# Attention outputs in two one-bank PSUM tiles, even transposes drained by two engines, later casts, and own slots for two early snapshots

## The chip, the cores and the metric

The kernel runs on one core of a Trainium2 chip. The metric is the device time of one execution in microseconds (us). Before the change the median of three runs is 999.97 us (998.2 to 1002.94). The engines are PE (TensorE), DVE (VectorE), ACT (ScalarE), POOL (GpSimd) and SP (SyncE, which here only issues DMAs). Each runs its own list of instructions in order and waits on semaphores for the others.

## The reference, cut to what matters

```
B, H, S, D = 4, 12, 448, 64
scores = q @ k.T / sqrt(D) - log(S);  attn = sigmoid(scores);  o = attn @ v        # 48 heads
x = o, heads joined                                                                # 1792 x 768
h = x @ w_in  (768 -> 2048);  g = elu(h);          x = g @ w_out  (2048 -> 768)    # first MLP
h = x @ w_in2 (768 -> 2048);  g = h - tanh(h);     out = g @ w_out2                # second MLP
```

All inputs are float32. The result has to be close to the fp32 one, so matrix products in the kernel are made from pairs of a rounded high part (type fp32r) and a low part that is the rest.

## The kernel before, in words

There are three stages, one behind the other: attention (0 to about 166 us), the first MLP, the second MLP. The two MLPs are nearly all of the time.

**Attention.** The 48 heads are 24 pairs, and a round m handles the pairs 2m (even) and 2m+1 (odd). For each pair k and q are loaded and transposed by PE through an identity (`transpose`, L325 to L329) into PSUM, copied to `plain` in SBUF (`drain`, L340 on ACT, L342 on DVE), rounded to a high part (`hi`, L352 on ACT for even pairs, L354 on DVE for odd ones) and a low part (`lo`, L358, DVE); both lie in the tile `e`. Three score groups of 18 matmul records follow (`s`, L377), each read by one sigmoid (`sig`, L398, ACT) that writes `an`. A remaining strip of both pairs has its own scores (`sr`, L388), sigmoid (`sig_rest`, L394) and value product (`pvr`, L415, in `pv_rest`). The value products (`pv`, L404) take 12 records for each pair, and `xdone` (L426, DVE) copies an output out of PSUM into x, which lies in R0a, R0b, R1a, R1b. PE's order in a round is: scores of the even pair, transposes of the next even and the next odd pair, scores of the odd pair, `pvr`, `sr` of the next round, `pv` of the even pair, `pv` of the odd pair.

PSUM in this stage: three tiles of two banks each form a ring (`ring`, L432 and after) that scores, odd transposes and `sr` use in turn. A fourth two-bank tile, tagged "o", is used in turn by the even transposes (`t_flat`, L316) and by the outputs of both pairs of a round (L408 and after: one half each). The tile framework makes a later writer of a tile wait for earlier readers of the same tile, whichever half they read.

Beside it, the MLP weights, which come in double-width words, are narrowed to float32 (L605 ACT, L608 and L612 DVE), summed (L665) and stored. These jobs load through SP's DMA queue all the time and fill ACT and DVE between the steps above.

**MLP.** Each product is split into blocks and done by seven block products P1 to P7 (a Strassen-Winograd scheme). Operand sums T1 to T4 of x are made by `x_sum` (L766), their high and low parts by `x_head` (L776, ACT) and `x_rest` (L782, DVE); `w_sum` (L725, mostly POOL), `w_head` (L739) and `w_rest` (L742) do the same for weights. `m_p` (L810) are the matmuls. `snap` (L822, ACT) copies a product out of its PSUM bank to SBUF when a later product must use the bank, `h_add` (L827), `g_sum` (L872) combine, `g_a`, `g_b`, `g_c` (L837, L843, L853) are the ELU. A step (i, g, s) is MLP i, block of columns g, half s of the tokens. Snapshots and partial sums live in numbered slots: slots 4 to 6 are `spare`, from 7 on they lie in R1b, 21 and 22 in the tile `first`, 23 to 25 in `second`. `RINGS` (L1227) lists which slots a step may use and `ring` (L1231) takes the one unused for longest. In step (0,0,1) the snapshot of P5, "s5", goes into the slot `i3` of R1b; R1b then still holds part of x, and the snapshot waits until the last `x_rest` that reads it is done.

**What sets the order.** Every operation is given a due time and a list of operations it depends on, and a planner sorts each engine's list by these. In attention the due times are the table `PHASES` (L114) with a period ROUND of 12000 per round. In the MLP they follow from planned costs. `sums_on` (L768) names the engine of an `x_sum`.

Of the kernel before, what the change touches and what calls it, by code (L numbers as in the profile page):

```python
# [16 lines left out]
class Sched:  # L17
# [94 lines left out]
ROUND = 2 * CYCLE  # L112
# [4 lines left out]
    "t": (1950 - ROUND, 2900 - ROUND), "plain": (2850 - ROUND, 3450 - ROUND), "hi": (4350 - ROUND, 5900 - ROUND), "lo": (5250 - ROUND, 6600 - ROUND),  # L117
# [4 lines left out]
SHIFTS = {(0, "ldv"): -12000, (0, "sr"): ROUND - 4700, (0, "sigr"): ROUND - 3900, (0, "ldvr"): -11000}  # L122


@with_exitstack
def kernel(
# [67 lines left out]
    with tc.manual_schedule():  # L194
# [7 lines left out]
        def attention():  # L202
# [76 lines left out]
            def when(kind, n, *rest):  # L279
                at = PHASES[kind]  # L280
# [5 lines left out]
                return n * ROUND + at + (0 if kind in ("s", "sig", "pv") else SHIFTS.get((n, kind), 0))  # L286
# [29 lines left out]
            def t_flat(n):  # L316
                if ("t", n) not in T:
                    p, tag = (pss[ring[("t", n)][0]], "s") if n % 2 else (pso, "o")
                    T["t", n] = p.tile([128, 2, BK], F32, tag=tag, name="sps").rearrange("p a t -> p (a t)")
                return T["t", n]  # L320

            def transpose(n):
                ps = t_flat(n)
                for c in range(3):
                    nc.tensor.transpose(ps[:, DD + c * 128:DD + (c + 1) * 128], kl[:, n % NL, c], ident)  # L325
                if n % 2 == 0:
                    nc.tensor.transpose(ps[:, :DD], krest[n // NR % 2][:, n // 2 % 2], ident)
                for c in range(R):
                    nc.tensor.transpose(ps[:, BK + c * SP:BK + (c + 1) * SP], ql[:, n % NL, c], ident[:SP, :SP])  # L329

            def parts_of(n):
                lo, hi = DD * (n % 2), DD + EW
                return [("ACT", lo, BK), ("DVE", BK, hi)] if n == 0 else [(("DVE", "ACT")[n % 2], lo, hi)]

            def drain(n, x):
                by, lo, hi = parts_of(n)[x]
                at = DD * (n % 2)
                out, in_ = plain[n % 2][:, lo - at:hi - at], t_flat(n)[:, lo:hi]
# [61 lines left out]
            def pv(n, u):  # L400
                m, x = divmod(n, 2)
                a = T.pop(("a", n, u))
                for j in range(2):
                    nc.tensor.matmul(  # L404
                        out=T["o", m][D * j:D * j + D, x, :S], lhsT=vl[m % NVL][:, x, 3 * j + u], rhs=a[:, j], start=False, stop=(u == 2), skip_group_check=True,
                    )

            def pv_rest(m):  # L408
                T["o", m] = pso.tile([128, 2, BK], F32, tag="o", name="pvps")
                a = T.pop(("a", m))  # L410
                for x in range(2):
                    n = 2 * m + x
                    for j in range(2):
                        lanes = slice(64 * x, 64 * x + 64)
                        nc.tensor.matmul(  # L415
                            out=T["o", m][D * j:D * j + D, x, :S], lhsT=vrest[n // NR % 2][lanes, m % (NR // 2), j], rhs=a[lanes, j], start=True, stop=False, skip_group_check=True,
                        )

            def xdone(n):
                b, hp = pairs[n]  # L420
                ps = T["o", n // 2][:, n % 2]
# [57 lines left out]
        def mlp():  # L479
# [288 lines left out]
            def sums_on(i, s, x):  # L768
                return "POOL" if (i, s) == (0, 1) and x in ("T3", "T4") else "DVE"
# [408 lines left out]
            def operands(i, s):  # L1178
# [22 lines left out]
                for x in ORDER:  # L1201
# [18 lines left out]
                    if x in SUMS:  # L1220
# [7 lines left out]
                     "g1": range(4), "gs": (23, 24, 25), "s10": range(4), "s11": (4, "i3", 0, 1, 2, 3), "r1": (5, 6)}  # L1228
            temps_free = {}

            def ring(kind, key, then, i=0):  # L1231
                turns[0] += 1
                slots = [t if isinstance(t, int) else 7 + 4 * i + int(t[1]) for t in RINGS[kind]]
                slot_of[key] = t = min(slots, key=lambda t: (used.get((kind[0], t), 0), slots.index(t)))
                used[kind[0], t] = turns[0]
                return tag_take(f"t{t}", then, stage_frees[1] if t >= 23 else scratch_free[0] if t >= 21 else temps_free["R1b"] if t >= 7 else stage_frees[3] if t >= 4 else before_early)

            def first_products(step):
# [14 lines left out]
                kind, kind_r = (f"s1{s}", "r1") if g == 0 else ("s2", "r")  # L1253
# [222 lines left out]
            for i in range(2):  # L1476
# [4 lines left out]
                for g in range(NG):  # L1481
                    first_weights(i, g)
                    for s in range(2):
                        first_products((i, g, s))
                room["R1b"] = [(0, RAW["R1b"], [d for t in range(7 + 4 * i, 11 + 4 * i) for d in turn_of.get(f"t{t}", [])])]
# [64 lines left out]
```

## Time and profile before

| | |
|---|---|
| runs | 999.97, 1002.94, 998.2 us |
| profiled execution | 998.61 us, its span 996.9 us |
| busy in the span | PE 968.8, DVE 766.8, ACT 603.3, POOL 113.8 us |
| mean granted TensorE clock | 0.996 of full speed |
| PE idle in front of `pv` (L404) | 9.5 us |
| longest wait of PE for ACT | 7.3 us, once, in front of L810 |
| DMA | 218.60 MB, 219 GB/s over the span |

The busy times are sums over the span; where they overlap they don't add up. A wait is named by the engine and the line that released it. Matmuls are pipelined, so the duration of one reaches into the next one, and the spacing of starts is the better price.

### The profile page before, as it was taken

How to read it: one execution, taken by the hardware profiler on the slowest of the kernel's cores; microseconds unless marked ns; L12 is line 12 of the kernel's file. 1: busy time of each engine (PE TensorE's matmuls, PEld its weight loads, DVE VectorE, ACT ScalarE, POOL GpSimd, SP SyncE). 2: the span in 40 equal slices, each digit the busy share in tenths (PEclk: the TensorE clock that was granted, in tenths of full speed). 3: DMA queues.
4: the chain of work that ended last, by engine and by line, in shares of the span. 5: the costliest groups of instructions: out<-in, count | busy, mean ns of one | idle time of the engine just before them, and what ended most of it. 6: DMA issues, size and time to landing. Idle time of an engine off the chain costs nothing.

```text
span 996.9 us, 15482 instructions
## 1 busy us (share of the span) xinstructions
PE 968.8 (97%) x5306; PEld 837.6 (84%) x5306; DVE 766.8 (77%) x1108; ACT 603.3 (61%) x940; POOL 113.8 (11%) x112
## 2 busy tenths in 40 slices
PE   7999999699999999999999998999999999999998
PEld 4555555688888888888899987899888999999998
DVE  4778888977888788778888898877777888666673
ACT  5778778666666677665666564444444565446652
POOL 2212210522222200000000201111111000000000
PEclk9999999899999999999999999999999999999999
DMA  8998870255555579999974725555555994455442
GB/s 252 317 350 299 279 260 35 86 186 193 193 193 188 187 252 353 390 399 370 365 252 148 231 75 180 177 192 185 182 192 188 328 328 135 126 171 175 126 146 85
DMA packets 144574, 218.60 MB, mean 219 GB/s; under 512 B 21424, under 2 KB 102896, under 8 KB 144240
## 3 DMA queue, kind: packets, MB, share of 16 engines
q1 hardware_dynamic: 143232, 217.10, 63.9%
q8 instruction: 41, 0.67, 0.3%
q10 hardware_dynamic: 1264, 0.52, 0.2%
q14 instruction: 37, 0.30, 0.1%
HBM read 142.61 MB, written 74.97 MB: 218 GB/s over the span
## 4 chain that ended last, share of the span: by engine, by line
PE 93%; DVE 3%; DMA 1%; issue 1%; ACT 1%; SPq 1%; POOL 0%; POOLq 0%; DVEq 0%; ACTq 0%
PE psa L810 12%; PE psd L810 11%; PE psx L810 10%; PE psu L965 7%; PE psv L965 7%; PE psw L965 7%; PE psa L965 6%; PE psb L965 6%; PE pvps L404 6%; PE psb L810 5%; PE psy L965 5%; PE sps L377 5%; PE psx L965 3%; PE psd L965 1%; PE pvps L415 1%
## 5 line engine op out<-in xcount | busy, mean ns | idle before, releaser
L398 ACT ACTIVATE an<-sps,bias 128x896 f32<-128x896 f32 x72 | 69.7, 1010 | 27.8 <-PE sps L377 27.5
L937 ACT ACTIVATE XB<-t 128x384 fp32r<-128x384 f32 (+1 forms) x111 | 62.1, 563 | 38.0 <-PE psw L965 11.5
L941 DVE TENSOR_TENSOR XB<-t,XB 128x384 fp32r<-128x384 f32 (+1 forms) x111 | 68.3, 625 | 10.6 <-ACT XB L937 10.5
L725 POOL TENSOR_TENSOR second<-second 128x384 f32<-128x384 f32 x15 | 19.2, 1279 | 500.0 <-DMA t<-x_forms 213.5
L404 PE MATMUL pvps<-an,vl 128*64 128x448 f32 x288 | 59.0, 546 | 9.5 <-DVE R0a L426 4.4
L404 PEld LDWEIGHTS pvps<-an,vl 128*64 128x64 f32 x288 | 19.4, 136 | 48.3 <-issue 32.1
L937 ACT ACTIVATE XB<-spare 128x512 fp32r<-128x512 f32 (+1 forms) x72 | 41.3, 574 | 29.7 <-PE psw L965 11.6
L810 PE MATMUL psa<-XB,W 128*128 128x512 f32 x192 | 54.2, 391 | 0.0
L941 DVE TENSOR_TENSOR XB<-spare,XB 128x512 fp32r<-128x512 f32 (+1 forms) x72 | 44.3, 621 | 10.1 <-ACT XB L937 9.8
L377 PE MATMUL sps<-e 64*128 64x448 f32 x432 | 51.1, 375 | 1.1 <-DVE e L354 0.5
L377 PEld LDWEIGHTS sps<-e 64*128 64x128 f32 x432 | 38.5, 184 | 14.5 <-issue 7.8
L965 PE MATMUL psu<-XB,XB 128*128 128x384 f32 (+1 forms) x192 | 46.3, 348 | 0.0
L965 PE MATMUL psv<-XB,XB 128*128 128x384 f32 (+1 forms) x192 | 46.2, 348 | 0.0
L965 PE MATMUL psw<-XB,XB 128*128 128x384 f32 (+1 forms) x192 | 46.1, 348 | 0.0
L810 PEld LDWEIGHTS psa<-XB,W 128*128 128x128 f32 x192 | 36.0, 188 | 7.5
L839 ACT ACTIVATE spare<-t 128x512 f32<-128x512 f32 (+1 forms) x33 | 19.0, 579 | 36.9 <-DVE t L827 35.9
L725 POOL TENSOR_TENSOR first<-first,second 128x384 f32<-128x384 f32 x30 | 41.0, 1366 | 1.2
L253 POOL COPY first<-raw_qk 128x384 f32<-128x384 f32 (+1 forms) x44 | 27.8, 657 | 106.6 <-PE sps L325 90.6
L810 PE MATMUL psd<-XB,W 128*128 128x512 f32 x144 | 35.6, 391 | 1.5 <-DVE W L742 1.3
L843 ACT ACTIVATE spare<-spare 128x512 f32<-128x512 f32 (+1 forms) x64 | 36.5, 572 | 0.8
L965 PE MATMUL psa<-XB,XB 128*128 128x384 f32 (+1 forms) x156 | 36.9, 347 | 0.0
L965 PE MATMUL psb<-XB,XB 128*128 128x384 f32 (+1 forms) x156 | 36.9, 347 | 0.0
(365 smaller groups left out, 2726.2 us busy)
## 6 DMA issues: line engine op xcount, KB each, us to landing
x_forms<-R1b SPq DMA_DIRECT2D x58, 256.0 KB, 2.0
first<-p_forms SPq DMA_DIRECT2D x36, 384.0 KB, 6.2
t<-x_forms SPq DMA_DIRECT2D x64, 192.0 KB, 3.0
t<-x_forms SPq DMA_DIRECT2D x47, 256.0 KB, 5.0
x_forms<-t SPq DMA_DIRECT2D x44, 256.0 KB, 2.0
x_forms<-R1b SPq DMA_DIRECT2D x58, 192.0 KB, 4.8
first<-in_moe_w_in_dram SPq DMA_DIRECT2D x14, 768.0 KB, 5.3
second<-in_moe_w_in_dram SPq DMA_DIRECT2D x14, 768.0 KB, 6.9
```

Of the source, the lines that this page charges most:

```text
L253: nc.gpsimd.tensor_copy(out=(ql, kl)[w][:, n % NL].rearrange("p c (h d) -> p c h d", h=2), in_=x)
L377: nc.tensor.matmul(out=ps[:, j, :S], lhsT=e[lanes, EW * kz + u * 128:EW * kz + (u + 1) * 128], rhs=e[lanes, EW * qz + KW:EW * qz + EW], st ...
L398: nc.scalar.activation(out=a, in_=T.pop(("s", n, u))[:, :, :S], func=ACTF.Sigmoid, bias=bias, scale=scale)
L404: nc.tensor.matmul(out=T["o", m][D * j:D * j + D, x, :S], lhsT=vl[m % NVL][:, x, 3 * j + u], rhs=a[:, j], start=False, stop=(u == 2), skip ...
L415: nc.tensor.matmul(out=T["o", m][D * j:D * j + D, x, :S], lhsT=vrest[n // NR % 2][lanes, m % (NR // 2), j], rhs=a[lanes, j], start=True, s ...
L725: by.tensor_tensor(out=out, in0=x, in1=y, op=op)
L810: nc.tensor.matmul(out=ps, lhsT=w[wz][:, k0:k0 + 128], rhs=xs[xz][:, kk], start=(opens and n == 0), stop=(n == 3 * KH - 1), skip_group_che ...
L839: nc.scalar.activation(out=r, in_=h, func=ACTF.Tanh)
L843: nc.scalar.activation(out=r, in_=r, func=ACTF.Exp, scale=-1.0)
L937: nc.scalar.activation(out=at_place(og_place[i, s, p, j], 0, i)[:, :HW[s]], in_=T["graw", i, s, p, j], func=ACTF.Copy)
L941: nc.vector.tensor_tensor(out=lo, in0=T.pop(("graw", i, s, p, j)), in1=f(hi), op=ALU.subtract)
L965: nc.tensor.matmul(out=T["o2", tag], lhsT=lhsT, rhs=rhs, start=(p in OPENS and j == 0 and x == 0), stop=(j == NG - 1 and x == 2), skip_gro ...
```

## The change

1. The fourth PSUM tile becomes two tiles of one bank each, "o0" and "o1" (new function `output`). The output of the even pair lies in o0 and that of the odd pair in o1. An even transpose has its k part in o0 and its q part in o1.
2. Even transposes are drained in two parts, 128x512 by ACT and 128x448 by DVE (before: 128x960 by DVE, but for pair 0). Odd ones are still drained by ACT.
3. The due times of `hi` and `lo` move: later for even pairs (from 4350 and 5250 to 6800 and 7700), earlier for odd pairs (from 5900 and 6600 to 4900 and 5500). Pairs 0 and 1 have corrections of their own.
4. The sums T3 and T4 of step (0,1) move from POOL to DVE.
5. The snapshots of step (0,0,1) use a ring of their own, "sa", of slots 4, 21, 22 and 3. "s5" then lies in slot 21 and "s2" in slot 22, both in `first`, which is used by other work afterwards; that work waits for them.

```diff
-    ... "hi": (4350 - ROUND, 5900 - ROUND), "lo": (5250 - ROUND, 6600 - ROUND),
+    ... "hi": (6800 - ROUND, 4900 - ROUND), "lo": (7700 - ROUND, 5500 - ROUND),
+FIRST_PAIRS = {(0, "hi"): -2450, (0, "lo"): -2450, (1, "hi"): 1000, (1, "lo"): 1100}
...
             def t_flat(n):
                 if ("t", n) not in T:
-                    p, tag = (pss[ring[("t", n)][0]], "s") if n % 2 else (pso, "o")
-                    T["t", n] = p.tile([128, 2, BK], F32, tag=tag, name="sps").rearrange("p a t -> p (a t)")
+                    if n % 2:
+                        ps = pss[ring[("t", n)][0]].tile([128, 2, BK], F32, tag="s", name="sps")
+                        T["t", n] = [ps[:, z] for z in range(2)]
+                        T["t", n, "all"] = ps.rearrange("p a t -> p (a t)")
+                    else:
+                        T["t", n] = [output(z) for z in range(2)]
                 return T["t", n]
+
+            def output(x):
+                return pso.tile([128, BK], F32, tag=f"o{x}", name=f"pv{x}")
...
             def parts_of(n):
                 lo, hi = DD * (n % 2), DD + EW
-                return [("ACT", lo, BK), ("DVE", BK, hi)] if n == 0 else [(("DVE", "ACT")[n % 2], lo, hi)]
+                return [("ACT", lo, hi)] if n % 2 else [("ACT", lo, BK), ("DVE", BK, hi)]
...
-                        out=T["o", m][D * j:D * j + D, x, :S], lhsT=vl[m % NVL][:, x, 3 * j + u], ...
+                        out=T["o", n][D * j:D * j + D, :S], lhsT=vl[m % NVL][:, x, 3 * j + u], ...
...
             def xdone(n):
                 b, hp = pairs[n]
-                ps = T["o", n // 2][:, n % 2]
+                ps = T["o", n]
...
             def sums_on(i, s, x):
-                return "POOL" if (i, s) == (0, 1) and x in ("T3", "T4") else "DVE"
+                return "DVE"
...
-                     "g1": range(4), "gs": (23, 24, 25), "s10": range(4), "s11": (4, "i3", 0, 1, 2, 3), "r1": (5, 6)}
+                     "g1": range(4), "gs": (23, 24, 25), "s10": range(4), "s11": (4, "i3", 0, 1, 2, 3), "sa": (4, 21, 22, 3), "r1": (5, 6)}
...
-                return tag_take(f"t{t}", then, ... scratch_free[0] if t >= 21 else ...)
+                return tag_take(f"t{t}", then, ... scratch_free[0] + stage_frees[0] if t >= 21 else ...)
...
-                kind, kind_r = (f"s1{s}", "r1") if g == 0 else ("s2", "r")
+                kind, kind_r = ("sa" if step == (0, 0, 1) else f"s1{s}", "r1") if g == 0 else ("s2", "r")
```

**Where it shows in the lists of instructions.** Lines of the changed kernel are numbered 12 higher from L340 on, so L404 there is L416. On PE, the value products of round 0, from the first output of the odd pair on, in the kernel before; the third row is the one that waits for DVE's copy:

```order
L404 MATMUL pvps<-an,vl_119 64x448 [waits DMAHW7_49]
L404 MATMUL pvps<-an,vl_119 64x448
L404 MATMUL pvps<-an,vl_119 64x448 [waits DVE_49,Activation_49]
L404 MATMUL pvps<-an,vl_119 64x448
L404 MATMUL pvps<-an,vl_119 64x448 [waits Activation_49]
```

and the same place in the changed kernel, where pv_284 is the tile o1:

```order
L416 MATMUL pv_284<-an,vl_119 64x448 [waits DMAHW7_49]
L416 MATMUL pv_284<-an,vl_119 64x448
L416 MATMUL pv_284<-an,vl_119 64x448 [waits Activation_49]
L416 MATMUL pv_284<-an,vl_119 64x448
L416 MATMUL pv_284<-an,vl_119 64x448 [waits Activation_49]
```

The wait for DVE is gone there, and the order of PE's matmuls is the same.

On ACT, one round of attention before (plain_122 is the odd pair's copy, e_83 the even pair's high part):

```order
L398 ACTIVATE an<-sps,bias 128x896 x3
L340 ACTIVATE plain_122<-sps 128x832
L352 ACTIVATE e_83<-plain_121 128x832
L398 ACTIVATE an<-sps,bias 128x896
L605 ACTIVATE XB_71<-XB_71 128x768
L398 ACTIVATE an<-sps,bias 128x896
L394 ACTIVATE ar<-sps,bias 128x896
L398 ACTIVATE an<-sps,bias 128x896
L605 ACTIVATE R1b<-R1a 128x768
```

and in the changed kernel:

```order
L410 ACTIVATE an<-sps,bias 128x896 x3
L352 ACTIVATE plain_121<-pv_359 128x512
L352 ACTIVATE plain_122<-sps 128x832
L410 ACTIVATE an<-sps,bias 128x896
L617 ACTIVATE XB_71<-XB_71 128x768
L410 ACTIVATE an<-sps,bias 128x896
L364 ACTIVATE e_83<-plain_121 128x832
L406 ACTIVATE ar<-sps,bias 128x896
L410 ACTIVATE an<-sps,bias 128x896
L617 ACTIVATE R1b<-R1a 128x768
```

A half drain of the even pair stands in front of the odd pair's drain, and the even pair's cast stands two places further back.

On DVE, the opening of the first MLP before, from the T2 sum on; the last row is the T4 rest, the last reader of x in R1b:

```order
L766 TENSOR_TENSOR R1a<-R1b,R1a 128x3x384
L827 TENSOR_TENSOR t<-t,psb 128x512
L827 TENSOR_TENSOR t<-t,psd 128x512
L827 TENSOR_TENSOR t<-t,psa 128x512
L782 TENSOR_TENSOR XB_1804<-R1a,XB_1804 128x1152
L853 SCALAR_TENSOR_TENSOR t<-spare,t 128x512 x2
L782 TENSOR_TENSOR XB_1804<-R1b,XB_1804 128x1152
L782 TENSOR_TENSOR XB_1804<-R1a,XB_1804 128x1152
L853 SCALAR_TENSOR_TENSOR t<-spare,t 128x512
L872 TENSOR_TENSOR t<-t 128x512
L742 TENSOR_TENSOR e_83<-first,e_83 128x768
L782 TENSOR_TENSOR R1a<-R1b,R1a 128x1152
```

and in the changed kernel, from the rest of T2 on, to the T4 rest and one row more:

```order
L794 TENSOR_TENSOR XB_1858<-R1a,XB_1858 128x1152 [waits Activation_49]
L778 TENSOR_TENSOR R1a<-R1a 128x3x384
L794 TENSOR_TENSOR XB_1858<-R1b,XB_1858 128x1152
L865 SCALAR_TENSOR_TENSOR t<-spare,t 128x512 [waits DVE_49,Activation_49]
L794 TENSOR_TENSOR XB_1858<-R1a,XB_1858 128x1152 [waits Activation_49]
L778 TENSOR_TENSOR R1b<-R1b,R1a 128x3x384
L754 TENSOR_TENSOR e_83<-first,e_83 128x768 [waits DMAHW2_49,PE_49,Activation_49]
L865 SCALAR_TENSOR_TENSOR t<-spare,psa 128x512 [waits Activation_49]
L839 TENSOR_TENSOR spare<-spare,psb 128x384
L794 TENSOR_TENSOR R1a<-R1b,R1a 128x1152 [waits Activation_49]
L839 TENSOR_TENSOR first<-first,psx 128x384 [waits PE_49]
```

Two sums (L778) have come in, and one ELU step (L853) and one `g_sum` (L872) less stand ahead of the T4 rest.

On ACT, the snapshot of P5 before, and what stands ahead of it:

```order
L776 ACTIVATE R1a<-R1b 128x1152 [waits DVE_49,Pool_49]
L843 ACTIVATE spare<-spare 128x512 [waits Activation_49]
L739 ACTIVATE W_1730<-second 128x768 [waits PE_49,Pool_49]
L822 ACTIVATE R1b<-psd 128x384 [waits DVE_49]
L837 ACTIVATE spare<-spare 128x384 [waits DVE_49]
```

and in the changed kernel:

```order
L788 ACTIVATE XB_1858<-R1a 128x1152 [waits DVE_49]
L751 ACTIVATE e_83<-first 128x768 [waits DMAHW2_49,PE_49]
L849 ACTIVATE spare<-psa 128x512 [waits DVE_49]
L834 ACTIVATE first<-psd 128x384 [waits PE_49]
L855 ACTIVATE spare<-spare 128x512 [waits Activation_49]
L834 ACTIVATE first<-psx 128x384 [waits PE_49]
```

The snapshot now goes into `first`, waits for PE alone, and stands ahead of the head of T4 (L788 R1a<-R1b), which follows two rows further on.

## Rows read from the trace of the kernel before

**Rows 1.** The page, part 1: busy us, share of the span, instructions.
```profile
PE 968.8 (97%) x5306; PEld 837.6 (84%) x5306; DVE 766.8 (77%) x1108; ACT 603.3 (61%) x940; POOL 113.8 (11%) x112
```

**Rows 2.** The page, part 5: busy, mean ns | idle before, releaser; the value products.
```profile
L404 PE MATMUL pvps<-an,vl 128*64 128x448 f32 x288 | 59.0, 546 | 9.5 <-DVE R0a L426 4.4
```

**Rows 3.** Timeline of PE in one round: start, duration, instruction [idle before <-releaser].
```profile
51.39 2.09 PE L377 MATMUL sps<-e 64*128 64x448 f32 x18
...
55.10 2.09 PE L377 MATMUL sps<-e 64*128 64x448 f32 x18
...
58.78 3.23 PE L404 MATMUL pvps<-an,vl 128*64 128x448 f32 x16
62.83 1.72 PE L404 MATMUL pvps<-an,vl 128*64 128x448 f32 x8 [0.82 <-DVE R0a L426]
```

**Rows 4.** Timeline of ACT in the same round, from the even pair's sigmoids on.
```profile
52.37 2.81 ACT L398 ACTIVATE an<-sps,bias 128x896 f32<-128x896 f32 x3 [4.17 <-PE sps L377]
55.20 0.87 ACT L340 ACTIVATE plain<-sps 128x832 f32<-128x832 f32 x1
55.97 0.90 ACT L352 ACTIVATE e<-plain 128x832 fp32r<-128x832 f32 x1
```

**Rows 5.** The drains' lines by form: ns min/median/max, starts, forms.
```profile
L340 ACT ACTIVATE plain<-sps x13: 597/871/872, 6.4 to 146.1; 128x832 f32<-128x832 f32 x12, 128x512 f32<-128x512 f32 x1
...
L342 DVE COPY plain<-sps x12: 625/1158/1159, 7.1 to 145.4; 128x960 f32<-128x960 f32 x11, 128x448 f32<-128x448 f32 x1
```

**Rows 6.** Stretches: us, then PE, PEld, DVE, ACT, POOL busy, PEclk, DMA share, GB/s.
```profile
100.00:150.00 50.00, 47.35 (x358) 26.83 (x356) 42.96 (x70) 39.12 (x47) 7.94 (x12) 1.00 0.82 267
12.00:150.00 138.00, 128.97 (x965) 72.41 (x963) 107.46 (x160) 107.57 (x127) 27.07 (x43) 1.00 0.91 302
...
190.00:200.00 10.00, 5.01 (x17) 5.01 (x18) 9.18 (x13) 5.38 (x9) 1.12 (x1) 0.66 0.40 152
```

**Rows 7.** Timeline of PE at the opening of the first MLP.
```profile
181.98 1.75 PE L810 MATMUL psb<-XB,e 128*128 128x384 f32 x9
183.56 1.73 PE L810 MATMUL psd<-R0b,W 128*128 128x384 f32 x9
185.79 1.86 PE L810 MATMUL psx<-XB,W 128*128 128x384 f32 x9 [0.50 <-ACT spare L822]
194.99 1.01 PE L810 MATMUL psd<-XB,R0a 128*128 128x384 f32 x2 [7.35 <-ACT R1b L822]
...
200.31 2.24 PE L810 MATMUL psa<-XA,e 128*128 128x512 f32 x9
202.39 0.51 PE L810 MATMUL psx<-R1a,e 128*128 128x384 f32 x2
```

**Rows 8.** Timeline of DVE there.
```profile
176.17 1.36 DVE L766 TENSOR_TENSOR R1a<-R1b,R1a 128x1152 f32<-128x1152 f32 x1
...
179.24 2.36 DVE L782 TENSOR_TENSOR XB<-R1a,XB 128x1152 fp32r<-128x1152 f32 x1
181.75 4.36 DVE L853 SCALAR_TENSOR_TENSOR t<-spare,t 128x512 f32<-128x512 f32 x2 [0.15 <-ACT spare L843]
...
188.13 2.14 DVE L782 TENSOR_TENSOR XB<-R1a,XB 128x1152 fp32r<-128x1152 f32 x1
...
193.07 1.35 DVE L782 TENSOR_TENSOR R1a<-R1b,R1a 128x1152 fp32r<-128x1152 f32 x1
194.34 0.68 DVE L853 SCALAR_TENSOR_TENSOR t<-spare,psa 128x512 f32<-128x512 f32 x1
...
195.54 0.54 DVE L827 TENSOR_TENSOR spare<-spare,psb 128x384 f32<-128x384 f32 x1
```

**Rows 9.** Timeline of POOL there: its first sum of x, its first sum of weights.
```profile
177.68 2.70 POOL L766 TENSOR_TENSOR R1a<-R1a 128x1152 f32<-128x1152 f32 x1 [41.87 <-DVE R1a L766]
...
184.09 1.47 POOL L725 TENSOR_TENSOR second<-second 128x384 f32<-128x384 f32 x1
```

**Rows 10.** Timeline of ACT there: the snapshot of P5.
```profile
194.45 0.49 ACT L822 ACTIVATE R1b<-psd 128x384 f32<-128x384 f32 x1 [1.67 <-DVE R1a L782]
```

More of the change, by code (lines that the diff above doesn't have):

```diff
@@ L116 @@
     "sr": 6600 - ROUND, "sigr": 7350 - ROUND,
-    "t": (1950 - ROUND, 2900 - ROUND), "plain": (2850 - ROUND, 3450 - ROUND), "hi": (4350 - ROUND, 5900 - ROUND), "lo": (5250 - ROUND, 6600 - ROUND),
+    "t": (1950 - ROUND, 2900 - ROUND), "plain": (2850 - ROUND, 3450 - ROUND), "hi": (6800 - ROUND, 4900 - ROUND), "lo": (7700 - ROUND, 5500 - ROUND),
     "side": (4500 - 2 * ROUND, 6000 - 2 * ROUND), "ldqk": (7000 - 3 * ROUND, 8500 - 3 * ROUND),
@@ L279, in when @@
             def when(kind, n, *rest):
-                at = PHASES[kind]
+                at, first = PHASES[kind], FIRST_PAIRS.get((n, kind), 0)
                 if kind not in ("sr", "sigr", "pvr", "ldk", "ldv", "ldqk1"):
@@ L285, in when @@
                     at = at[rest[0]]
-                return n * ROUND + at + (0 if kind in ("s", "sig", "pv") else SHIFTS.get((n, kind), 0))
+                return n * ROUND + at + first + (0 if kind in ("s", "sig", "pv") else SHIFTS.get((n, kind), 0))
             def loads(m):
@@ L337, in drain @@
                 at = DD * (n % 2)
-                out, in_ = plain[n % 2][:, lo - at:hi - at], t_flat(n)[:, lo:hi]
+                out = plain[n % 2][:, lo - at:hi - at]
+                if n % 2:
+                    in_ = T["t", n, "all"][:, lo:hi]
+                else:
+                    in_ = t_flat(n)[lo // BK][:, lo % BK:(hi - 1) % BK + 1]
                 if by == "ACT":
@@ L404, in pv @@
                     nc.tensor.matmul(
-                        out=T["o", m][D * j:D * j + D, x, :S], lhsT=vl[m % NVL][:, x, 3 * j + u], rhs=a[:, j], start=False, stop=(u == 2), skip_group_check=True,
+                        out=T["o", n][D * j:D * j + D, :S], lhsT=vl[m % NVL][:, x, 3 * j + u], rhs=a[:, j], start=False, stop=(u == 2), skip_group_check=True,
                     )
             def pv_rest(m):
-                T["o", m] = pso.tile([128, 2, BK], F32, tag="o", name="pvps")
                 a = T.pop(("a", m))
@@ L412, in pv_rest @@
                     n = 2 * m + x
+                    T["o", n] = output(x)
                     for j in range(2):
@@ L415, in pv_rest @@
                         nc.tensor.matmul(
-                            out=T["o", m][D * j:D * j + D, x, :S], lhsT=vrest[n // NR % 2][lanes, m % (NR // 2), j], rhs=a[lanes, j], start=True, stop=False, skip_group_check=True,
+                            out=T["o", n][D * j:D * j + D, :S], lhsT=vrest[n // NR % 2][lanes, m % (NR // 2), j], rhs=a[lanes, j], start=True, stop=False, skip_group_check=True,
                         )
@@ L1235, in ring @@
                 used[kind[0], t] = turns[0]
-                return tag_take(f"t{t}", then, stage_frees[1] if t >= 23 else scratch_free[0] if t >= 21 else temps_free["R1b"] if t >= 7 else stage_frees[3] if t >= 4 else before_early)
+                return tag_take(f"t{t}", then, stage_frees[1] if t >= 23 else scratch_free[0] + stage_frees[0] if t >= 21 else temps_free["R1b"] if t >= 7 else stage_frees[3] if t >= 4 else before_early)
             def first_products(step):
@@ L1484, in mlp @@
                         first_products((i, g, s))
+                        if (i, g, s) == (0, 0, 1):
+                            scratch_free[0] += turn_of["t21"] + turn_of["t22"]
                 room["R1b"] = [(0, RAW["R1b"], [d for t in range(7 + 4 * i, 11 + 4 * i) for d in turn_of.get(f"t{t}", [])])]
```

6 lines of the change are left out of this document (3 added, 3 removed).

## The prediction, made before the changed kernel was run

> **What bounds the kernel now.** I read four views in this order. The busy shares: PE works 968.8 of 996.9 us [rows 1], so all that the change can give back is in the 28 us in which PE stands, or in work that PE does at a lower clock. The groups by cost, then, with the idle time in front of each: 9.5 us of PE's idle time stand before the value products and are put down to DVE's copies of attention outputs [rows 2]. The timelines of one round of attention and of the opening of the first MLP: in the round PE stops for 0.82 us between the 16th and the 17th record of the value products, released by DVE's copy of the even pair's output [rows 3]; at the opening it stops once for 7.35 us, released by a snapshot on ACT [rows 7], which waited for a rest on DVE [rows 10]. Last the stretches: from 190 to 200 us the granted clock is 0.66 of the 2.4 GHz, behind that long stop, and DMA is busy for 0.91 of the stretch from 12 to 150 us [rows 6].
>
> **Part 1, two PSUM tiles.** The 17th record writes the odd pair's half while the copy reads the even pair's half. With two tiles the wait has no cause, and the changed list of PE doesn't have it. All ten waits are of this kind, so 9.5 us go [rows 2]. What could be late instead: records 17 to 24 also need the odd pair's second and third sigmoid, which I place with part 2; and the next even transposes need both copies out of the way, as before, with one score group of about 2.1 us [rows 3] between the last value product and them, while such a copy is short beside it. I cost that at nothing; if the cover were gone, a copy's length, about 0.6 us by the 128x448 copy on DVE [rows 5], would come back each round.
>
> **Part 2, drains.** DVE gives up 1158 ns per even pair for 625 ns, off PE's path. ACT takes over a 128x512 drain of 597 ns [rows 5], ahead of the odd pair's drain. One ACT copy hands over to the next 0.10 us before its end (55.20 + 0.87 against 55.97) [rows 4], so the odd drain moves back by about 0.50 us, its end from 56.07 to 56.57. It frees the ring tile for the third score group of the odd pair. Those 18 records begin at 55.10 and take 2.0 us from start to start, a third of it 0.67 [rows 3], so the third group wants to begin at 56.45. Before there is 0.38 us in hand; afterwards about 0.2 us is missing with the semaphore's way: 11 rounds with an odd drain in them, 2.2 us. Bounds: 0, if the three even sigmoids come earlier by the 0.1 to 0.2 that is missing (ACT sits idle up to 4.17 us before them [rows 4], but that idle is PE's pace), and 5.5 us (all of 0.50 in each of 11 rounds). I take 2.2.
>
> **Part 3, later and earlier casts.** The even pair's cast moves behind two sigmoids and a narrowing, at about 59.2 us by adding rows of 0.9 to 1.0 us each; with its low part it is done by about 62 us, against about 63.7 at which the next round would start without the 0.82 us (62.83 + 1.72 - 0.82) [rows 3]. Cost nothing, 1.5 us in hand; without it, each 0.1 us late costs 1.1 us. The third odd sigmoid goes back by the same 0.50 us as the drain; value products that read it are the last four of the 24 and have some 0.8 us in hand. So attention gives 9.5 - 2.2 = 7.3 us, bounded by 9.5 and 9.5 - 5.5 = 4.0, or less if transfers pace it (a rival).
>
> **Parts 4 and 5, the opening of the MLP.** Before, P6 starts at 185.79 and the products are 1.58 us apart (181.98 to 183.56) [rows 7]. P3 has to wait until P5's snapshot has left the bank, and that waits for the rest of T4, which reads R1b and ends at 194.42 [rows 8, 10]. With a slot in `first` it needs PE's product alone. ACT's list has it ahead of T4's head. So P3 follows P6 at 187.37, P7 at 188.95, and the next psa product at 190.53 instead of 200.31 [rows 7]: 9.8 us, of which 7.35 are the stop, and 2.2 the lower clock (P3 and P7 took 200.31 - 194.99 = 5.3 us instead of 3.2).
>
> What is late next is P4, which uses T4's rest (the psx product on R1a at 202.39 [rows 7], after 2.08 us of psa): it is wanted at 192.6. DVE's chain to that rest, counted from the rest at 179.24: it was 15.2 us long [rows 8]. Six POOL operations ran beside it from 177.68 to 191.1 [rows 6, 9], and stretched three rests from 1.35 to 2.14 to 2.36 (together 2.6 us) and the pair of ELU steps from 2 x 0.68 to 4.36 (3.0 us) [rows 8]. Unstretched that is 9.6. Added: two sums at 1.36 [rows 8], 2.7. Less by the order: one ELU step (0.68) and one `g_sum` of the same shape, more one `h_add` of 0.54; together 0.8 off. That is 11.5, without POOL. POOL keeps four weight sums of 1.47 [rows 9], 5.9 us; at the rate seen, 5.6 us of stretch in 13.4 us of POOL, they cost 2.5. The rest of T4 ends at 179.24 + 14.0 = 193.2, and one `h_add` behind it, 0.54, frees psx: 193.8. P4 waits 1.2 us. Bounds of this wait: 0 (no stretch: 191.3) and 4.6 us (each us of POOL one of DVE: 197.2). I take 1.2, so the opening gives 9.8 - 1.2 = 8.6 us, bounded by 9.8 and 5.2.
>
> The row shows that DVE and POOL slow each other but both run: 5.6 us lost to 13.4. The Trainium skill, "SBUF — State Buffer", section "SBUF: two separate sides", says that the port pair shared by VectorE and GpSimd is an exclusive lock and that "the other fully blocks" where VectorE reads two SBUF inputs. By that rule all of POOL's four sums would stand in DVE's way, P4 would wait near the 4.6 us of the upper bound, and the sum would be 986.1 instead of 982.7. The stretch of less than half agrees with turns between two that are both busy as well as with sharing, so the trace doesn't decide it here.
>
> The slots 21 and 22 were free at that time; what uses `first` next is narrowing for weights that are needed later. I cost this at nothing; if it were late, it would show as a wait of PE for a weight rest. The second MLP's opening has the same instructions but for its sums' neighbours: nothing.
>
> **The sum,** against the profiled execution of 998.61 us, which is 1.4 us under the median of 999.97: 998.61 - 7.3 - 8.6 = 982.7. The spread of the three runs, 4.7 us, is about 0.5%, and less than 0.5% I call no change.
>
> **Rivals.**
> - *The opening pays, attention does not.* Transfers run 0.91 of the time from 12 to 150 us at 302 GB/s [rows 6]. If the narrowing jobs that sit between the sigmoids on ACT arrive as late as before in absolute time, ACT stands before them, and the waits move from the copies to the sigmoids. For it: the high share. Against it: from 100 to 150 us the share is 0.82, and PE still stops for copies. Attention then gives 0 to 2 us: 998.61 - 8.6 - 1 = 989.0.
> - *Attention pays, the opening blocks anew.* DVE is the only engine left with the chain to T4's rest; the two sums it takes over come on top, and POOL's weight sums fall in the same time. With the wait of 4.6 us: 986.1; if snapshots and h_adds behind it are held as well and the opening gives nothing, 991.3. I put it at 987. For it: DVE is busy for 9.18 of the 10 us to 200 [rows 6]. Against: POOL's share is cut by more than half.
> - *Slower: the transfers decide all of attention.* 138 us at 302 GB/s are 41.7 MB. In the last 50 us only 267 GB/s came through [rows 6]. If the tighter order of work makes loads and stores meet such that the whole stretch gets 267, those bytes take 156 us: 18 us more, less 8.6 of the opening: 1008. It ends above the time before from a rate of about 284 GB/s on (147 us). Against it: nothing that is transferred changes, and the low rate of the last stretch goes with a share of 0.82, so engines had time left.
> - *The wait is not the false one.* If records 17 to 24 waited in truth for the sigmoid, with the copy only last by little, part 1 gives half, 4.7: 987.3. The released-by column names DVE in all ten, so I fold it into the first.
>
> **How the numbers follow.** The forecast, 982.7, has 0.65; the first rival 0.19, the second 0.12, the slower one 0.04. The forecast's own ends are 998.61 - 9.5 - 9.8 = 979.3 and 998.61 - 4.0 - 5.2 = 989.4. The first rival reaches to about 992. I give 977 to 993: below 979.3 for a change in the clock or in waits that I don't see, above for the first two rivals; this leaves out the slower case and the edges of the others. Faster by over 0.5% means under 995.0: 0.65 + 0.19 x 0.9 + 0.12 x 0.8 = 0.91, and I say 0.90. Within 0.5%: 0.06; slower: 0.04.
>
> **What will show it.** Right: no idle before the value products put down to `xdone`; rounds that had a stop are 0.6 to 0.8 us shorter; the third odd score group waits 0.1 to 0.3 us for ACT's drain; P3 starts within 1 us after P6; the granted clock stays near 1.00 there; P4 waits 0 to 2 us for DVE. Wrong: value products that wait for sigmoids, ACT standing before narrowing with a DMA as releaser, score groups that wait for the even low part, or a stop of over 4 us before P4 or P3.

## The result and the profile after

The changed kernel takes 985.66 us (median of four runs, 983.11 to 987.84) against 999.12 us before (four runs): a ratio of 0.9857 over all runs (0.9865 by the two medians), 95% interval 0.9819 to 0.9896. The profiled execution took 987.84 us, with a span of 985.8 us. The forecast was 982.7 us, so 3 us of the forecast gain are missing, and in the profiled execution 5. The profile shows that this small difference is the rest of two larger ones of opposite sign.

The page of the changed kernel, part 1, answers [rows 1]: PE has lost 12 of its 28 us of idle time.

```profile
PE 969.9 (98%) x5306; PEld 837.6 (85%) x5306; DVE 762.4 (77%) x1110; ACT 610.3 (62%) x951; POOL 107.8 (11%) x110
```

What PE still waits for, all of the changed kernel's span (us in total, times, longest):

```profile
PE psd L822 <- DVE W L754: 2.4, 2, 1.3
PE psy L977 <- ACT XB L949: 2.0, 1, 2.0
...
PE sps L333 <- ACT an L410: 0.9, 1, 0.9
...
PE sps L389 <- ACT plain L352: 0.7, 2, 0.4
```

The copies of attention outputs are not in the list any more, and neither is the 7.3 us wait for the snapshot. In the MLPs two stops are new: one of the two waits for a weight rest (the other, 1.28 us at the opening of the second MLP, was there before), and psy, the first group of output products. In attention, waits of an odd transpose for a sigmoid (`an`) and of the odd score groups for ACT's drain (`plain`) are new, 1.6 us together.

A round of attention on PE (start, duration, instruction), beside [rows 3]: the 24 value products run through, and the odd pair's score group takes 2.18 for 2.09 us. From its start to the start of the next scores, `pv` takes 4.67 us (54.98 to 59.65) instead of 5.70 (58.78 to 64.48 before), so a stop of 0.82 us of idle time cost 1.03.

```profile
47.50 2.09 PE L389 MATMUL sps<-e 64*128 64x448 f32 x18
...
51.20 2.18 PE L389 MATMUL sps<-e 64*128 64x448 f32 x18
...
54.98 4.73 PE L416 MATMUL pv<-an,vl 128*64 128x448 f32 x24
59.65 2.09 PE L389 MATMUL sps<-e 64*128 64x448 f32 x18
```

The opening of the first MLP on PE, beside [rows 7]: P6, P3, P7 (from 179.60), the next psa product and P4 follow without a stop.

```profile
157.29 2.34 PE L822 MATMUL psa<-XA,e 128*128 128x512 f32 x9
...
176.48 1.72 PE L822 MATMUL psx<-XB,W 128*128 128x384 f32 x9
178.04 0.51 PE L822 MATMUL psd<-XB,R0a 128*128 128x384 f32 x2
...
181.16 2.24 PE L822 MATMUL psa<-XA,e 128*128 128x512 f32 x9
183.24 0.51 PE L822 MATMUL psx<-R1a,e 128*128 128x384 f32 x2
```

DVE there, beside [rows 8]: the T4 rest (180.73) ends at 182.08 and the `h_add` that frees psx at 182.54, 0.7 us before P4 starts.

```profile
171.07 2.13 DVE L794 TENSOR_TENSOR XB<-R1a,XB 128x1152 fp32r<-128x1152 f32 x1
173.12 1.35 DVE L778 TENSOR_TENSOR R1a<-R1a 128x1152 f32<-128x1152 f32 x1
...
180.73 1.35 DVE L794 TENSOR_TENSOR R1a<-R1b,R1a 128x1152 fp32r<-128x1152 f32 x1
182.00 0.54 DVE L839 TENSOR_TENSOR first<-first,psx 128x384 f32<-128x384 f32 x1
```

POOL there, beside [rows 9]: its weight sums are over when the first moved sum starts on DVE.

```profile
167.02 1.93 POOL L737 TENSOR_TENSOR second<-second 128x384 f32<-128x384 f32 x1 [35.44 <-DMA second<-kept_wi]
168.91 1.01 POOL L737 TENSOR_TENSOR first<-first,second 128x384 f32<-128x384 f32 x1
169.88 1.01 POOL L737 TENSOR_TENSOR second<-second,first 128x384 f32<-128x384 f32 x1
170.97 1.01 POOL L737 TENSOR_TENSOR first<-first,second 128x384 f32<-128x384 f32 x1
```

**Where the time is, by four marks.** M0 is the first psa product of the first MLP (165.57 before), M1 the psa product behind the opening (200.31 before [rows 7], 181.16 now), M2 the first stop in the second MLP, which every kernel here has (psx waits 0.96 us for a snapshot; the two rows below, before and now). A mark read on PE's timeline in each profile makes the experiments comparable, since PE's order of matmuls from M0 on is the same in all of them.

```profile
601.81 1.84 PE L810 MATMUL psx<-XB,W 128*128 128x384 f32 x9 [0.96 <-ACT R1b L822]
588.81 1.84 PE L822 MATMUL psx<-XB,W 128*128 128x384 f32 x9 [0.96 <-ACT R1b L834]
```

| profile | to M0 | M0 to M1 | M1 to M2 | M2 to the end | span |
|---|---|---|---|---|---|
| before | 165.6 | 34.7 | 401.5 | 395.1 | 996.9 |
| changed | 157.3 | 23.9 | 407.6 | 397.0 | 985.8 |
| difference | -8.3 | -10.9 | +6.2 | +1.9 | -11.1 |

Attention and the opening gave 19.2 us, more than the 15.9 that were forecast. Then 6.2 us were given back in the rest of the first MLP, where the forecast had nothing. This is where, on PE, in the output products:

```profile
378.00 0.84 PE L977 MATMUL psw<-XB,XA 128*128 128x512 f32 x3
380.88 0.49 PE L977 MATMUL psy<-XB,XA 128*128 128x512 f32 x1 [2.03 <-ACT XB L949]
381.61 1.21 PE L977 MATMUL psy<-XB,XA 128*128 128x512 f32 x2 [0.23 <-DVE XB L953]
382.61 1.49 PE L977 MATMUL psa<-XB,XA 128*128 128x512 f32 x3
383.89 1.40 PE L977 MATMUL psb<-XB,XA 128*128 128x512 f32 x3
385.13 0.84 PE L977 MATMUL psy<-XB,XA 128*128 128x512 f32 x3
```

Groups of three are 0.68 us apart, so the last of these rows would start at 378.00 + 4 x 0.68 = 380.72; it starts at 385.13, 4.4 us late. Half of it is the stop. The other half is the clock behind it, granted at 0.71 from 380 to 384 us (PE, PEld, DVE, ACT, POOL busy, PEclk, DMA share, GB/s):

```profile
376.00:380.00 4.00, 2.84 (x13) 2.03 (x11) 1.54 (x4) 1.78 (x3) 0.00 (x0) 1.00 1.03 394
380.00:384.00 4.00, 2.89 (x7) 2.12 (x8) 2.81 (x4) 3.34 (x6) 0.00 (x0) 0.71 1.04 392
```

The other part of the 6.2 us is a stop of psd for a weight rest, 1.07 us of idle time at 214.32, with the matmuls around it 1.6 us (its third record starts at 214.32; 0.23 apart, counted on from the group before, it would be 212.72). The last 1.9 us, behind M2, are no part of the change: they follow from a low clock behind a 1.28 us stop that the kernel before has as well, and the third kernel of the last set, which has attention and opening as before, has them in its profile, while the second profile of the changed kernel does not.

### The profile page after: what moved, and what is told of

It is laid out like the page before. It is cut to its first block, busy times and chain, and to the rows that moved or that the text cites. A ratio compares the mean times of both kernels' runs of the same rounds, so it can differ in the third digit from the quotient of the medians.

```text
span 985.8 us, 15460 instructions
## 1 busy us (share of the span) xinstructions
PE 969.9 (98%) x5306; PEld 837.6 (85%) x5306; DVE 762.4 (77%) x1110; ACT 610.3 (62%) x951; POOL 107.8 (11%) x110
## 4 chain that ended last, share of the span: by engine, by line
PE 93%; DMA 3%; DVE 2%; ACT 1%; SPq 1%; issue 1%; POOL 0%; DVEq 0%; ACTq 0%; POOLq 0%
PE psa L822 13%; PE psd L822 12%; PE psx L822 10%; PE psu L977 6%; PE psv L977 6%; PE psw L977 6%; PE psa L977 6%; PE psb L977 6%; PE psb L822 6%; PE pv L416 5%; PE psy L977 5%; PE sps L389 4%; PE psx L977 3%; PE psd L977 1%; DMA R1a<-in_moe_w_in_dram 1%; PE pv L427 1%
## 5 line engine op out<-in xcount | busy, mean ns | idle before, releaser
L416 PE MATMUL pv<-an,vl 128*64 128x448 f32 x288 | 56.8, 544 | 0.0
L416 PEld LDWEIGHTS pv<-an,vl 128*64 128x64 f32 x288 | 19.5, 136 | 36.5 <-issue 30.7
L254 POOL COPY first<-raw_qk 128x384 f32<-128x384 f32 (+1 forms) x44 | 36.4, 852 | 93.8 <-DMA raw_qk<-in_k_dram 74.2
L977 PEld LDWEIGHTS psu<-XB,XB 128*128 128x128 f32 x192 | 34.7, 188 | 2.1 <-DVE XB L942 0.2
```

Of the source, the lines that this page charges most:

```text
L254: nc.gpsimd.tensor_copy(out=(ql, kl)[w][:, n % NL].rearrange("p c (h d) -> p c h d", h=2), in_=x)
L416: nc.tensor.matmul(out=T["o", n][D * j:D * j + D, :S], lhsT=vl[m % NVL][:, x, 3 * j + u], rhs=a[:, j], start=False, stop=(u == 2), skip_gr ...
L977: nc.tensor.matmul(out=T["o2", tag], lhsT=lhsT, rhs=rhs, start=(p in OPENS and j == 0 and x == 0), stop=(j == NG - 1 and x == 2), skip_gro ...
```

## The experiments

All are edits of the changed kernel unless it is said otherwise. Times are medians of up to five rounds beside the kernel before on the same chip; a ratio is to that kernel, over all runs, and can differ by up to 0.002 from that of the two medians.

**The first set: the changed kernel again, its two halves, and the DMA queue.** Unedited:

> The changed kernel again, for its spread and a second profile. Theory 1 (a new stop behind the first MLP's input products, 2.0 + 0.2 us of idle time before psy and some 2 us at a lower granted clock behind it, gives back part of the gain every time): the stop is there again at about 381 us, and runs lie at 983 to 988. Theory 2 (what was given back is an accident of one execution, the clock above all): the stop or the low clock is missing in this profile, and most runs lie near 982.

Measured: 985.99 us (983.24 to 986.80), ratio 0.9856 (0.9839 to 0.9874). The stop before psy is there, 3.02 us, with the clock at 0.83 from 380 to 390 us. It belongs to the kernel, as theory 1 has it; the 1.9 us behind M2 don't (395.4 here). Runs lie from 983 to 988 in both sets.

Parts 4 and 5 undone:

```diff
-                return "DVE"
+                return "POOL" if (i, s) == (0, 1) and x in ("T3", "T4") else "DVE"
...
-                kind, kind_r = ("sa" if step == (0, 0, 1) else f"s1{s}", "r1") if g == 0 else ("s2", "r")
+                kind, kind_r = (f"s1{s}", "r1") if g == 0 else ("s2", "r")
```

(and the two places where slots 21 and 22 are handed on).

> The changed kernel with the sums T3 and T4 of step (0,1) back on POOL and the two snapshots in the old ring: only the attention parts are left. Theory 1 (attention alone gives about 8.3 us, by the profiles 165.57 to 157.29 at the first MLP product): 990 to 991, and the stop of about 7.3 us before P3 is there, released by the snapshot into R1b. Rival (the two halves overlap: with attention faster the T4 rest comes relatively later and the stop grows): 993 or more, with a stop above 8 us.

Measured: 987.90 us, ratio 0.9887 (0.9869 to 0.9904). That is 2 us better than theory 1, and the rival is out. M0 is at 155.97, the stop before P3 is the old one, and between M1 and M2 there is no stop at all:

```profile
175.59 1.84 PE L822 MATMUL psx<-XB,W 128*128 128x384 f32 x9 [0.26 <-ACT spare L834]
184.79 1.01 PE L822 MATMUL psd<-XB,R0a 128*128 128x384 f32 x2 [7.37 <-ACT R1b L834]
...
189.41 2.24 PE L822 MATMUL psa<-XA,e 128*128 128x512 f32 x9
```

So attention alone carries 12 of the 13.8 us of these rounds (999.75 to 985.99), and the whole of the opening's 10.9 us are worth 2 us in the end.

The kernel before with parts 4 and 5 alone, the same lines the other way round:

> The kernel before with parts 4 and 5 alone (sums on DVE, own slots for the two snapshots). Theory 1 (the opening alone gives about 10.9 us by 200 us, of which the stop behind the input products takes little since PE arrives there less early): 988 to 990. Rival (the sum of the halves is all there is, and the loss at 381 us belongs to this half): 992 to 993, with a stop of 2 us or more before psy.

Measured: 1001.54 us, ratio 1.0002 (0.9987 to 1.0018): nothing, though single runs lie from 995.10 to 1002.56, wider than elsewhere. Theory 1 is wrong by the whole gain. M0 to M1 takes 25.5 us instead of 34.7, as wanted; but M1 to M2 takes 411.0 instead of 401.5, with these two stops:

```profile
226.14 2.32 PE L810 MATMUL psd<-XB,W 128*128 128x512 f32 x7 [2.57 <-DVE W L742]
```

and 2.27 us before psy. PE comes here 12 us later than in the changed kernel, so being early isn't what makes it wait. The rival had the place right (this half) and the size too small.

Double-width w_out loads begun six output units later:

```diff
-                        p, j = divmod(2 + 3 * n, NG)
+                        p, j = divmod(8 + 3 * n, NG)
```

> The changed kernel with the double-width w_out loads of the second MLP begun six output units later (8 + 3n for 2 + 3n). Theory 1 (the load of 128x1536 double words into R1a, issued at 370.87 ahead of three reloads that the first output products need, makes these late): the stop before psy at 381 us goes, and the time is 3 to 4.5 us under the changed kernel's in the same rounds. Rival (DMA is 1.04 busy there, the rate sets when the operands come, whatever the order): the stop stays at 1.5 us or more and the time is within 1 us of the changed kernel's.

Measured: 982.06 us (981.44 to 982.86), ratio 0.9822 (0.9808 to 0.9837); 3.9 us under the changed kernel of the same rounds, and under every run of it. The stop is 0.91 us, and the clock stays at 1.00. In the changed kernel the queue shows why: the 128x1536 load into R1a (768 KB) stands ahead of three of the four reloads of g into t (256 KB each) issued from 370 to 376 us, and ACT's heads wait for those.

```profile
370.00 0.32 SPq L946 DMA_DIRECT2D t<-x_forms  x1
370.87 0.33 SPq L606 DMA_DIRECT2D R1a<-in_moe_w_out_dram  x1
372.36 0.32 SPq L946 DMA_DIRECT2D t<-x_forms  x1
...
374.09 0.32 SPq L946 DMA_DIRECT2D t<-x_forms  x1
```

```profile
377.95 0.63 ACT L949 ACTIVATE XB<-t 128x512 fp32r<-128x512 f32 x1 [2.52 <-DMA t<-x_forms]
...
380.20 0.63 ACT L949 ACTIVATE XB<-t 128x512 fp32r<-128x512 f32 x1 [0.41 <-DMA t<-x_forms]
```

The DMA share is 1.00 to 1.06 in either kernel at this place, so it is the order in the queue that decides, not the rate alone. The kernels with old slots agree: there the same load, the first of w_out into R1a, is issued behind four reloads of g into t. In the kernel without part 5, below, that is 3.4 us ahead of psy, which starts at 382.35 without a stop:

```profile
378.96 0.53 SPq L606 DMA_DIRECT2D R1a<-in_moe_w_out_dram  x1
```

In the changed kernel it is 7.8 us ahead of 378.68, where psy would have started. This version has the lowest median of the study.

**The second set: each part undone by itself.** Part 5 undone, the sums left on DVE (the `kind` line above):

> The changed kernel without part 5: the snapshots of step (0,0,1) in the old ring, the two sums on DVE. Theory 1 (the own slots in `first` hold up the narrowing of the next weights, and that is what the changed kernel pays for later): P3 stands 4 to 5 us, until DVE has done the T4 rest, but the stops at 214 us (weight rest) and 381 us (psy) are gone, and from the first psa product behind the opening to the next MLP's first stop it takes 401 to 402 us as before, not 407 to 409; the time is 984 to 986. Rival (those stops come from PE being early, or from the sums on DVE): they stay, and the time is 988 or more.

Measured: 985.52 us, ratio 0.9866 (0.9852 to 0.9880): the same as the changed kernel. The opening costs three short stops, 4.4 us in all,

```profile
175.87 2.04 PE L822 MATMUL psd<-R0b,W 128*128 128x384 f32 x9 [2.16 <-DVE t L839]
177.71 3.08 PE L822 MATMUL psx<-XB,W 128*128 128x384 f32 x9
181.84 0.62 PE L822 MATMUL psd<-XB,R0a 128*128 128x384 f32 x2 [1.05 <-ACT R1b L834]
...
184.89 0.62 PE L822 MATMUL psx<-XB,R0a 128*128 128x384 f32 x2 [1.22 <-ACT t L834]
```

and M1 to M2 takes 401.5 us, with no stop. Theory 1 holds, but for the form of the stop, which is split in three. With the loads where they are, part 5 is worth nothing: it wins 6.8 us before M1 (30.7 to 23.9) and loses 6.2 to 7.2 behind it.

Part 4 undone, the own slots left (the `sums_on` line above):

> The changed kernel without part 4: the own slots, but the sums T3 and T4 on POOL. Theory 1 (the slots cause the later stops): a weight rest is waited for at 210 to 225 us by 1 us or more and psy by 1 us or more. P3 does not stand; P4 waits 3 to 8 us for the T4 rest, since POOL's sums take 2.7 and 3.8 us beside a busy DVE. Time 988 to 993. Rival (the sums on DVE cause the later stops): no stop at 214 and 381, and a time of 983 to 986.

Measured: 989.41 us, ratio 0.9898 (0.9884 to 0.9911). M1 to M2 takes 407.4 us and psy stops for 2.43; so the slots are what makes psy late, whoever does the sums. (All of its 5.9 us over 401.5 stand here: the 2.43, and slower matmuls behind the stop, at a clock of 0.50 from 384 to 388 us.) The stop for a weight rest is not there, against theory 1; it needs the sums on DVE too. In the opening it is P3 that waits, 3.84 us, and not P4.

The even transposes' k part drained by DVE as well:

```diff
-                return [("ACT", lo, hi)] if n % 2 else [("ACT", lo, BK), ("DVE", BK, hi)]
+                return [("ACT", lo, hi)] if n % 2 else [("ACT" if n == 0 else "DVE", lo, BK), ("DVE", BK, hi)]
```

> The changed kernel with both parts of the even transposes drained by DVE (two copies, 128x512 and 128x448), but for pair 0. Theory 1 (ACT's share makes the odd drain 0.5 us later, for which the third odd score group pays 0.1 to 0.25 us a round, and DVE has room): attention 1 to 3 us shorter, the third group's 18 records take 2.09 again and not 2.18. Rival (DVE's later casts then are late and the even low part holds the next scores): attention 3 us longer or more, PE waiting for DVE e.

Measured: 991.87 us, ratio 0.9925 (0.9913 to 0.9937), 6 us worse, and not by attention: M0 is at 157.0, and it lies between 155.2 and 158.2 in all kernels with two tiles. The odd score group takes 2.28 us in six rounds here, longer than the 2.18 of the changed kernel, so this run doesn't show that ACT's drain is what it pays for. With the old cast times it is 2.18 in most rounds with ACT's drain (the next experiment) and 2.09 in most rounds with DVE's (part 1 alone, in the third set). So the small price of ACT's drain is there with the old cast times; with the new ones DVE's drains are no cheaper, and nothing of either is seen at M0. The 6 us are behind M0: 25.2 to M1, and in M1 to M2, 412.2 us, with a stop of 2.57 for a weight rest at 217.14 and one of 2.23 before psy. The opening parts in the kernel before (first set) have nearly the same two stops, 2.57 and 2.27, and 411.0 us; there DVE drains the even transposes too. The planner sets the first MLP's order from planned costs, and this edit moved it: the lists of DVE and ACT behind M0 are no longer the changed kernel's, but nearly those of that other kernel. Own slots cost 9.5 to 10.7 us behind M1 in these two, 6 to 7 in the kernels with ACT's drains. I did not follow that further. Both theories were about the wrong place.

The old cast times:

```diff
-    ... "hi": (6800 - ROUND, 4900 - ROUND), "lo": (7700 - ROUND, 5500 - ROUND),
+    ... "hi": (4350 - ROUND, 5900 - ROUND), "lo": (5250 - ROUND, 6600 - ROUND),
...
-FIRST_PAIRS = {(0, "hi"): -2450, (0, "lo"): -2450, (1, "hi"): 1000, (1, "lo"): 1100}
+FIRST_PAIRS = {}
```

> The changed kernel with the old due times of hi and lo. Theory 1 (the later even cast takes ACT's time out of the place between the odd drain and the fourth sigmoid; with the old one the fourth sigmoid starts 0.9 us later, and the value products of the odd pair wait for the sixth): attention 2 to 8 us longer, PE waiting for ACT an. Rival (part 3 moves work within idle time): within 1 us of the changed kernel.

Measured: 986.17 us, ratio 0.9862 (0.9846 to 0.9878), M0 at 158.2: the rival holds, part 3 is within the spread.

**The third set: the rest of the stop, two controls, and part 1 alone.** The loads still later (`divmod(min(12 + 3 * n, 55), NG)`):

> The changed kernel with the double-width w_out loads ten output units later than in it (12 + 3n, at most 55, for 2 + 3n; the earlier experiment had 8 + 3n). Theory 1 (what stops psy is the place of these loads in the DMA queue): the 0.9 us that were left of the stop go too, time 981 to 982. Rival (the rest of the stop has another cause, the reloads being issued late): 0.9 us stay, time 982 to 983.

Measured: 982.69 us, ratio 0.9837 (0.9824 to 0.9851). Before psy 0.2 us are left, M1 to M2 takes 404.1 us (405.0 in the earlier experiment). The whole stop is the queue's, as theory 1 says; the time lies in the rival's range, and in time the two kernels with later loads can't be told apart. What remains over 401.5 is mostly the stop for the weight rest, 1.07 us.

The later loads (8 + 3n) without part 5, and then in the kernel before:

> The changed kernel without part 5 and with the double-width loads at 8 + 3n. Theory 1 (without the own slots nothing stops psy, so there is nothing to be gained by the later loads): within 1 us of the kernel without part 5, 985 to 986. Rival (the later loads help any of these kernels, by less traffic beside the products): 982 to 984.

> The kernel before with nothing but the double-width loads at 8 + 3n. Theory 1 (no stop before psy there, so nothing to gain): 998.5 to 1000, no change. Rival: 995 to 997.

Measured: 984.78 us, ratio 0.9858 (0.9845 to 0.9872), against 985.52 without the later loads; and 999.30 us, ratio 1.0000 (0.9991 to 1.0009). Later loads give nothing clear of the spread where no stop is. And part 5 does pay once the loads are out of the way: in the same rounds 982.69 us with it (12 + 3n) and 984.78 without it (8 + 3n), and no run of the one reaches the other. M1 to M2 is 401.5 us in both. The second one's profile has 397.1 us behind M2, with the clock at 0.92 from 600 to 620 us: the accident of the changed kernel's first profile.

Part 1 alone (parts 2 to 5 undone by the edits above; the even transposes need two copies on DVE since they lie in two tiles):

> Part 1 alone: two one-bank tiles, even transposes drained by DVE in two copies, old cast times, old slots, sums on POOL. Theory 1 (the false wait is what attention paid, the drains and casts matter little): first MLP product at 155 to 158 us, the stop of 7.3 us before P3 stays, time 988 to 991. Rival (without the earlier drains and later casts other waits take the place of the removed one): first MLP product at 161 us or later, time 994 or more.

Measured: 990.47 us, ratio 0.9914 (0.9901 to 0.9928), M0 at 156.43: all that attention gives up to M0 comes from the two tiles. Between M0 and M1 it takes 35.0 us, with the old stop of 7.37 and one of 0.97 for a weight rest at 166.32, which the second experiment (parts 1 to 3) doesn't have. That one has 33.4 us there and the lower time, 0.9887 against 0.9914, so parts 2 and 3 seem to add some 2 us behind M0; the intervals of the two just touch. Parts 2 to 5 together add 5 to 6 us (0.9914 to 0.9857; 990.47 to 985.66 us).

The marks of the experiments on which the verdicts rest:

| profile | own slots | sums on | M0 | M0 to M1 | M1 to M2 |
|---|---|---|---|---|---|
| before | no | POOL | 165.6 | 34.7 | 401.5 |
| attention parts only | no | POOL | 156.0 | 33.4 | 401.5 |
| part 1 alone | no | POOL | 156.4 | 35.0 | 401.5 |
| without part 5 | no | DVE | 155.9 | 30.7 | 401.5 |
| without part 4 | yes | POOL | 155.3 | 29.6 | 407.4 |
| opening parts only | yes | DVE | 165.7 | 25.5 | 411.0 |
| changed, first and second profile | yes | DVE | 157.3, 156.9 | 23.9, 23.9 | 407.6, 408.7 |
| changed, loads at 8 + 3n, 12 + 3n | yes | DVE | 155.2, 156.3 | 23.9, 23.9 | 405.0, 404.1 |

The last column is 401.5 in every kernel with the old slots, and 404 to 412 in every one with own slots (the one with DVE's drains has 412.2, the one with the old cast times 408.0).

## Why the prediction was right, and the step that failed

The time fell into the range, and the direction was forecast. Step by step:

- *Part 1, the false wait: right.* No value product waits for a copy, and part 1 alone brings M0 forward by 9.1 us; 9.5 were forecast. That figure was idle time; from start to start a stop of 0.82 us cost 1.03.
- *Part 2, the later odd drain: right in kind.* The odd score group pays 0.1 us in most rounds, and PE stops for nearly 0.4 in two. Summed over eleven rounds, from the start of the odd group to the next instruction's, it is 2.4 us more than before in this profile, but 0.9 to 1.1 in three others with the same attention (the changed kernel again, attention alone, loads at 8 + 3n); 2.2 were forecast. So the size was near in one profile and twice too large in the others. That ACT's drain is the cause is shown with the old cast times only.
- *Part 3: at nothing, as forecast.*
- *Attention together: 8.3 us for 7.3.* In the other profiles with the same attention M0 lies from 155.2 to 156.9, so it gave up to 10.4. The transfer rival shows on PE in one round only: a narrowing on ACT waits 2.15 us for its load, and an odd transpose behind it 0.89 for a sigmoid.
- *Parts 4 and 5, the opening: right in mechanism, mis-sized.* It gave 10.9 us for 8.6, by P4's start as well as by M1. From P6 to the next psa product the forecast 9.8 us are there (200.31 - 185.79 = 14.5 before, 181.16 - 176.48 = 4.7 now). Another 1.0 us came ahead of P6 (M0 to P6 takes 19.2 instead of 20.2), where the stop of 0.50 us before P6 was among what went and the forecast had nothing. The term that was off is the wait before P4, 1.2 us forecast and none seen, since DVE's chain from the T2 rest to the T4 rest took 11.0 us (171.07 to 182.08) and not 14.0. The stretch of DVE by POOL was 0.8 us for 2.5: one rest took 2.13 instead of 1.35, since POOL's four sums ran from 167 to 172, ahead of most of the chain. The chain without POOL was forecast at 11.5 and is 10.2; 0.8 of that is an ELU step which POOL had stretched before and which the forecast did not count as stretched:

```profile
190.19 1.48 DVE L853 SCALAR_TENSOR_TENSOR t<-spare,t 128x512 f32<-128x512 f32 x1
```

  So the upper bound that went with the Trainium skill's exclusive lock ("SBUF — State Buffer", section "SBUF: two separate sides") was not put to the test here.
- *"What uses `first` next is narrowing for weights that are needed later. I cost this at nothing": wrong, by 6 to 7 us.* The sign named there, a wait of PE for a weight rest, is what came, with a second stop 170 us later. The narrowing writes its scratch into the room of slots 21 and 22, and so has to wait until what lies there has been stored. In the kernel without part 4 the profile names that wait:

```profile
199.52 0.92 ACT L617 ACTIVATE first<-first 128x768 f32<-128x768 f32 x1 [0.53 <-DMA x_forms<-first]
```

  Counted from M1, it starts on ACT 10.5 us behind in the kernel before (210.83), in the kernel with attention alone (199.93) and without part 5 (197.08), but 17.2 us behind in the changed kernel (198.40). Its load was issued 5.7 us behind M1 there (186.90) and 2.7 in the kernel before, so 3 of these 6.7 us come ahead of the load. On ACT in the changed kernel,

```profile
198.40 0.90 ACT L617 ACTIVATE first<-first 128x768 f32<-128x768 f32 x1
```

  and on SP there, its load and the stores out of these slots (the second of the two stores, issued at 193.4, landed 4.9 us later, at 198.3, and the narrowing started at 198.40; it also stands on ACT just behind an instruction that waited 1.76 us for another store of this line, and which of the two held it here can't be told):

```profile
186.90 0.38 SPq L606 DMA_DIRECT2D first<-in_moe_w_in_dram  x1
...
192.28 1.41 SPq L888 DMA_DIRECT2D x_forms<-first  x2
```

  POOL's sums of these weights then begin 24.9 us behind M1 (206.02) instead of 17.5, and the rests stand behind them. That own slots cause the loss behind M1 is shown by the last table; that the queue's order makes the stop before psy, by the two kernels with later loads. The way from the late narrowing to the weight rest at 214 us is read from this profile alone. How own slots come to put the load ahead of the reloads in the planned order was not tried, and stays open.

So the forecast was near partly by luck, as two misses of opposite sign cancelled: 3.3 us too little before M1, and 6.2 us not seen behind it.

## What to carry to other kernels

A tile that two writers share makes false waits whatever half they touch; a finer tile is worth trying before the order is, and here it alone made 9 of the 13 to 14 us. A slot that is free now is not free of cost: look up who takes it next, how early that work starts, and who stands behind that, above all where the order is planned and one later start moves a queue. Mark three or four places on the bottleneck engine and compare the intervals: a gain that is given back 200 us later shows at once in such a table, and the sum over the span hides it.

## What the runs showed of the hardware that was not expected

- The same stop costs differently from run to run. Behind 1.28 us of idle time at the opening of the second MLP the granted clock stayed at 1.00 in the profile before (613 to 621 us) and was 0.63 from 604 to 608 in the changed kernel; the price was 1.9 us.
- POOL and DVE slowed each other here as well: between 206 and 211 us, with POOL's sums at 1.34 instead of 1.01 us, a `g_sum` on DVE took 1.50 us instead of 0.69 and an ELU step 1.36 instead of 0.55, and the weight rest that PE waited for stood behind them.
